# A Strassen gate/up projection moved from float32r to scaled fp16 sums

## The chip, the cores and the metric

The kernel runs on one core of a Trainium2 chip. The metric is device time in microseconds (us) of one execution. A core's engines run side by side, each taking its own instructions in order: TensorE (PE; its weight loads are listed as PEld), VectorE (DVE), ScalarE (ACT), GpSimd (POOL) and SyncE (SP, which here only issues DMA). Matmul results land in PSUM banks; other data lies in SBUF.

## The reference, cut to what matters

```python
# S = 2048 rows, D = 1024, F = 3584, 32 heads; inputs in bfloat16, scaled by 0.05
xn  = layernorm(x)
s   = linear_attention(xn, wqkv) @ wo            # phi(q) phi(k)^T v, normalised
g   = silu( (silu(xn @ w_gate) * (xn @ w_up)) @ w_down )
out = x + s * g
```

The two products `xn @ w_gate` and `xn @ w_up` ("gate/up") are the largest part.

## The kernel before

The kernel goes through these stages: layer norm, keys and values; the "query stage" (queries, attention and the output projection, four blocks of 512 rows; block 0 is the first, and its numerators are computed between the query products of the next); then two passes over 1,024 rows each, a pass being gate/up followed by down. Weights stream in. Gate/up uses one level of Strassen's method (Winograd's form): a group of 256 columns of `w_gate` or `w_up` is cut into 2x2 blocks, and seven products of sums of blocks stand in for eight. Each product is four matmuls of 512 columns, so a group is 28 matmuls, there are 28 groups in a pass, and a pass is 784 matmuls.

The weights' sums T1 to T4, the activations' sums S1, S2, S3 and a copy of one plain block (A22, which meets T4) are kept in float32r, a 32-bit format that TensorE multiplies; S4 and the plain operands are 16-bit. The T sums are made in pass 1 on GpSimd, stored to DRAM in 32 bits, and loaded again in pass 2:

```python
def t_pair():
    return [tp.tile([P, 2, HK, P], F32R, name="T%d" % k, tag="T") for k in range(2)]   # tp: 8 buffers
def emit_T(key, w):
    b11, b12 = w[:, 0:HK, 0:P], w[:, 0:HK, P:2 * P]
    b21, b22 = w[:, HK:DC, 0:P], w[:, HK:DC, P:2 * P]
    ...
    nc.gpsimd.tensor_tensor(out=T1, in0=b12, in1=b11, op=ALU.subtract)
    nc.gpsimd.tensor_tensor(out=T2, in0=b22, in1=T1, op=ALU.subtract)
    ...
...
# the products of a group, first half; y_, x_ and zw are PSUM banks
prod(y_[:], lambda k: T2[:, k, :], lambda k: S2[:, k, :], True)
prod(x_[:], lambda k: w[:, k, 0:P], lambda k: x1[:, k, :], True)
prod(zw[:, 0, :], lambda k: T3[:, k, :], lambda k: S3[:, k, :], True)
prod(zw[:, 1, :], lambda k: T1[:, k, :], lambda k: S1[:, k, :], True)
nc.scalar.copy(out=s1[:], in_=x_[:])
nc.vector.tensor_tensor(out=s2[:], in0=y_[:], in1=s1[:], op=ALU.add)
nc.vector.tensor_tensor(out=s3[:], in0=zw[:, 0, :], in1=s2[:], op=ALU.add)
```

The end of a row block, in the last sweep of down. `io` holds a block of 128 rows of `x` and of `s`, and takes one of the eight buffers of the pool of T:

```python
io = tp.tile([P, 2, D], BF16, name="io", tag="T")
xres, s_in = io[:, 0, :], io[:, 1, :]
nc.sync.dma_start(out=xres, in_=x2[r0:r0 + P, :])
nc.sync.dma_start(out=s_in, in_=s_dram[r0:r0 + P, :])
...                                                  # the matmuls of this row block
nc.scalar.activation(out=sy[:], in_=ys[(t, cc)][...], func=ACT.Silu)
nc.vector.tensor_tensor(out=sy[:], in0=sy[:], in1=s_in[:, cs], op=ALU.mult)
nc.vector.tensor_tensor(out=xres[:, cs], in0=sy[:], in1=xres[:, cs], op=ALU.add)
eng = nc.sync if last else nc.gpsimd
eng.dma_start(out=out2[r0:r0 + P, cs], in_=xres[:, cs])
```

Of the kernel before, what the change touches and what calls it, by code (L numbers as in the profile page):

```python
# [21 lines left out]
def kernel(  # L22
# [39 lines left out]
    NPREP = 12  # L62

# [9 lines left out]
    wgu = ctx.enter_context(tc.tile_pool(name="wgu", bufs=3))  # L73
    tp = ctx.enter_context(tc.tile_pool(name="tp", bufs=8))
# [19 lines left out]
    make_identity(nc, ident[:])  # L94
    mask = persist.tile([P, P], FP32, name="mask")
# [25 lines left out]
    t_drams = {}  # L121
# [29 lines left out]
    def emit_Q(b, g):  # L151
        if b not in pqT_tiles:
            pqT_tiles[b] = blk12.tile([P, G, TB], BF16, name="pqT", tag="pqT")
        pqT = pqT_tiles[b]
        btok = slice(b * TB, (b + 1) * TB)
        q_ps = ps2.tile([P, TB], FP32, name="q_ps", tag="B2")
        for dc in range(DC):
            nc.tensor.matmul(q_ps[:], lhsT=wq_sb[:, dc, g * P:(g + 1) * P], rhs=xn_ap(dc, btok),  # L158
                             start=(dc == 0), stop=(dc == DC - 1))
        emit_phi(phiw, q_ps[:], pqT[:, g, :], TB, in_place=True, act=b > 0 or g % 2 == 1)  # L160

    NPASS = NB // 2
    passes = list(range(NPASS - 1, -1, -1))
    w_seq = []
    for p in passes:
        for fg in range(NFG):
            w_seq.append((p, "g", fg))
            w_seq.append((p, "u", fg))
        for sw in range(2):
            for q in range(FC // 2):  # L170
                w_seq.append((p, "d%d" % sw, q))
    w_tiles = {}
    w_next = [0]
    n_slot = [0]
    first_gate = [None]

    def w_slot():
        t = wgu.tile([P, DC, FW], BF16, name="w_sb", tag=("wg_sb" if n_slot[0] % 2 == 0 else "wu_sb"))
        n_slot[0] += 1
        return t  # L180

    def load_gu(t, kind, k, after=None):
        d = nc.sync.dma_start(out=t[:], in_=(wg_v if kind == "g" else wu_v)[:, :, k * FW:(k + 1) * FW])
        gate([d], after, sync=True)

    def load_w(after=None):
# [6 lines left out]
        if kind[0] == "d":  # L193
            nc.sync.dma_start(out=t[:].rearrange("p a b -> p (a b)").rearrange("p (k n) -> p k n", k=2),
                              in_=wd_v[:, 2 * k:2 * k + 2, :])
        else:
            load_gu(t, kind, k, after or first_gate[0])
# [6 lines left out]
    t_tiles = {}  # L204

    def t_pair():
        return [tp.tile([P, 2, HK, P], F32R, name="T%d" % k, tag="T") for k in range(2)]

    def emit_T(key, w):
        b11, b12 = w[:, 0:HK, 0:P], w[:, 0:HK, P:2 * P]  # L210
        b21, b22 = w[:, HK:DC, 0:P], w[:, HK:DC, P:2 * P]
        ta, tb = t_pair()
        T2, T1, T3, T4 = ta[:, 0], ta[:, 1], tb[:, 0], tb[:, 1]
# [4 lines left out]
        g = key[1:]  # L218
        if g not in t_drams:
            t_drams[g] = [dram.tile([P, 2, HK, P], FP32, name="t%d_%s%d" % (k, key[1], key[2])) for k in range(2)]  # L220
            for src, dst in zip((ta, tb), t_drams[g]):
                nc.gpsimd.dma_start(out=dst[:], in_=src[:].bitcast(FP32))
        t_tiles[key] = (T1, T2, T3, T4)

    def load_T(key):
        ta, tb = t_pair()
        for dst, src in zip((ta, tb), t_drams[key[1:]]):
            gate([nc.sync.dma_start(out=dst[:].bitcast(FP32), in_=src[:])], first_gate[0], sync=True)
        t_tiles[key] = (ta[:, 1], ta[:, 0], tb[:, 0], tb[:, 1])

    gkeys = [(passes[0], kd, fg) for fg in range(NFG) for kd in ("g", "u")]
    prep_q = deque(gkeys[2:2 + 2 * NPREP:2] + gkeys[0:2])

    def prep(n, after=None):
        for _ in range(n):
            if not prep_q:
                return
            key = prep_q.popleft()
            t = w_slot()
            load_gu(t, key[1], key[2], after)  # L240
            emit_T(key, t)
            if key in gkeys[0:2]:
                w_tiles[key] = t
            else:
                t_tiles.pop(key)

    kvz_ps = [psA.tile([P, GPT, NDW], FP32, name=f"kvz{j}", tag="A") for j in range(NJ)]
    with ExitStack() as p1:
# [8 lines left out]
        p1_man.enter_context(tc.manual_schedule(engines={mybir.EngineType.PE, mybir.EngineType.DVE,  # L257
                                                         mybir.EngineType.Activation, mybir.EngineType.Pool,
                                                         mybir.EngineType.SP}))
        NXP = (NT + 1) // 2  # L260
        xp_tiles = [wgu.tile([P, 2, D], BF16, name="xp", tag=("wg_sb" if k % 2 == 0 else "wu_sb"))
                    for k in range(NXP)]

        def x_ap(i):
            return xp_tiles[i // 2][:, i % 2, :]
# [170 lines left out]
        for k in range(NWARM):  # L436
            nc.tensor.matmul(wps[:], lhsT=warm[:, 0:P], rhs=warm[:], start=True, stop=True)
        emit_stats(0)
# [30 lines left out]
        for i in range(2, NT):  # L469
            for c in range(NCH):  # L470
# [5 lines left out]
                emit_Bev(i, c)  # L476
                if c % 2 == 1:
# [8 lines left out]
            if i >= 8:  # L486
                prep(1)
        emit_C(NT - 1)
        ps1.close()
        ps2 = p12.enter_context(tc.tile_pool(name="ps2", bufs=5, space=PSUM, reuse_waits="tile"))  # L490
        for g in range(G):
            emit_Q(0, g)
            if g % 4 == 3:
# [4 lines left out]
    p2_man.enter_context(tc.manual_schedule(engines={mybir.EngineType.PE, mybir.EngineType.DVE,  # L498
                                                     mybir.EngineType.Activation, mybir.EngineType.Pool,
                                                     mybir.EngineType.SP}))  # L500
    for j in range(NJ):
        g0 = j * GPT
        ng = min(GPT, G - g0)
        nc.vector.tensor_tensor(out=KVZ[:, g0:g0 + ng, 0:P], in0=kvz_ps[j][:, 0:ng, 0:P],
                                in1=mask[:, None, :].to_broadcast([P, ng, P]), op=ALU.mult)
        nc.vector.tensor_tensor(out=KVZ[:, g0:g0 + ng, P:P + HPG],
                                in0=kvz_ps[j][:, 0:ng, P:P + 1].to_broadcast([P, ng, HPG]),
                                in1=sel[:, None, :].to_broadcast([P, ng, HPG]), op=ALU.mult)

    s_sums = {}  # L510

    def emit_Ssum(p):
# [4 lines left out]
        S1, S2, S3, A22 = [sp.tile([P, HK, TB], F32R, name="S%d" % k, tag="S%d" % k) for k in range(4)]  # L517
        S4 = sp.tile([P, HK, TB], F16, name="S4", tag="S4")
# [4 lines left out]
        nc.scalar.copy(out=A22[:], in_=a22)  # L523
        s_sums[p] = (S1, S2, S3, S4, A22)

    with ExitStack() as p2:
# [82 lines left out]
        for b in range(NB):  # L609
            q = [q_item(b + 1, g) for g in range(G)] if b + 1 < NB else []  # L610
            sl = sh(b - 1, 0) + sh(b - 1, 1) if b > 0 else []
            body = q[:2] + mix(q[2:], sl)
            at = (1, 4, 7, 10) if len(body) > 12 else ((1, 3, 5, 7) if b == 0 else (0, 1, 2, 3))
# [9 lines left out]
        prep(len(prep_q))  # L623
# [5 lines left out]
    with ExitStack() as p3:  # L629
        kp = p3.enter_context(tc.tile_pool(name="p3k", bufs=8, reuse_waits="tile"))  # L630
        cp_ = p3.enter_context(tc.tile_pool(name="p3c", bufs=1, reuse_waits="tile"))
        hp = p3.enter_context(tc.tile_pool(name="p3h", bufs=1, reuse_waits="tile"))
# [14 lines left out]
        def emit_a(key):  # L647
            p = key[0]
            w, (T1, T2, T3, T4) = w_tiles[key], t_tiles[key]
            S1, S2, S3, S4, A22 = s_sums[p]  # L650
            x1 = xn_blk_tiles[2 * p]
            y_ = pps.tile([P, TB], FP32, name="yb", tag="s")
# [7 lines left out]
            nc.scalar.copy(out=s1[:], in_=x_[:])  # L660
            nc.vector.tensor_tensor(out=s2[:], in0=y_[:], in1=s1[:], op=ALU.add)  # L661
            nc.vector.tensor_tensor(out=s3[:], in0=zw[:, 0, :], in1=s2[:], op=ALU.add)  # L662
            grp[key] = [x_, zw, s2, s3, None]

        def emit_c22(key):
            p, kind, fg = key
            x_, zw, s2, s3, _ = grp[key]
            if kind == "g":
                dst = s3[:]
            else:  # L670
                c = cp_.tile([P, 4, TB], FP32, name="cu", tag="cu")
                grp[key][4] = c
                dst = c[:, 3, :]
            nc.vector.tensor_tensor(out=dst, in0=zw[:, 1, :], in1=s3[:], op=ALU.add)

        def emit_b(key, last=False):
            w, (T1, T2, T3, T4) = w_tiles[key], t_tiles.pop(key)
            S1, S2, S3, S4, A22 = s_sums[key[0]]
# [4 lines left out]
            prod(zw[:, 0, :], lambda k: T4[:, k, :], lambda k: A22[:, k, :], False)  # L683
# [4 lines left out]
        def emit_evac(key, h):  # L688
            p, kind, fg = key
            x_, zw, s2, s3, c = grp.pop(key)  # L690
            if kind == "g":
                c = xnp.tile([P, 4, TB], FP32, name="sg", tag="xn8")
                sg_tiles[(p, fg)] = c
            nc.vector.tensor_tensor(out=c[:, 1:3, :], in0=zw[:], in1=s2[:, None, :].to_broadcast([P, 2, TB]),  # L694
                                    op=ALU.add)
            if kind == "g":
                nc.scalar.activation(out=c[:, 3, :], in_=s3[:], func=ACT.Silu)
                nc.scalar.activation(out=c[:, 1:3, :], in_=c[:, 1:3, :], func=ACT.Silu)  # L698
                nc.scalar.activation(out=c[:, 0, :], in_=x_[:], func=ACT.Silu)
# [139 lines left out]
```

## Time and profile before

The time is 801.97 us, the median of three runs (801.56 to 803.89). The profiled execution spans 799.1 us on the core. The stages, cut at the starts of matmuls, are:

| stage | us |
|---|---|
| start, keys and values | 128.74 |
| query stage | 117.80 |
| gate/up, pass 1 | 177.15 |
| down, pass 1 | 96.50 |
| gate/up, pass 2 | 177.15 |
| down, pass 2 (to the end of its last matmul) | 96.85 |
| after the last matmul's end | 4.90 |

The next fence has the page's totals of the kernel before: busy time of each engine, its share of the span and its instructions, and under it the shares of the chain of work that ended last.

```profile
PE 790.2 (99%) x3787; PEld 431.3 (54%) x3787; DVE 453.0 (57%) x739; ACT 232.9 (29%) x384; POOL 215.5 (27%) x357
PE 96%; DVE 2%; ACT 0%; DMA 0%; issue 0%; DVEq 0%; ACTq 0%
```

TensorE is the bound: busy in 99% of the span, and 96% of the chain.

Next are four of the stages of the kernel before (query, gate/up of pass 1, gate/up of pass 2, and what follows the last matmul), one line each: window, its length in us, then busy us (and instructions) of PE, PEld, DVE, ACT and POOL, the granted clock, the DMA engines' busy share, and GB/s.

```profile
128.74:246.54 117.80, 117.80 (x644) 57.45 (x641) 73.88 (x188) 69.86 (x120) 41.10 (x43) 1.00 0.64 176
246.54:423.69 177.15, 177.15 (x787) 112.85 (x786) 120.22 (x137) 47.34 (x72) 76.68 (x81) 1.00 0.78 250
520.19:697.35 177.16, 177.16 (x787) 112.86 (x786) 121.66 (x141) 44.67 (x71) 1.49 (x3) 1.00 0.81 265
794.20:799.10 4.90, 0.00 (x1) 0.00 (x0) 2.07 (x5) 0.66 (x2) 0.00 (x0) 0.76 0.25 80
```

In both gate/up stages PE is busy for the whole length, so they can only become shorter by matmuls that follow each other sooner. Which ones could, the groups by line and shape show (kernel before; operation, output<-inputs, shapes, count | busy us, mean ns of one | idle time before them):

```profile
L641 PE MATMUL yb<-S,T 128*128 128x512 f32 x224 | 71.5, 441 | 0.0
L641 PEld LDWEIGHTS zw<-S,T 128*128 128x128 f32 x672 | 126.4, 188 | 32.3
L641 PEld LDWEIGHTS <-w_sb 128*128 128x128 bf16 x672 | 56.8, 98 | 83.1 <-issue 30.5
```

A weight load takes 188 ns in float32r and 98 ns in 16 bits. One group of 28 matmuls, on TensorE's timeline of the kernel before (start us, busy us, engine, line, operation, output<-inputs, shape, count; `yb` is the product with T2 and opens a group):

```profile
395.54 1.28 PE L641 MATMUL yb<-S,T 128*128 128x512 f32 x4
396.67 1.04 PE L641 MATMUL xb<-xnT,w_sb 128*128 128x512 bf16 x4
397.35 3.12 PE L641 MATMUL zw<-S,T 128*128 128x512 f32 x12
400.31 1.04 PE L641 MATMUL zw<-S,w_sb 128*128 128x512 f16 x4
401.18 1.03 PE L641 MATMUL xb<-xnT,w_sb 128*128 128x512 bf16 x4
401.86 0.58 PE L641 MATMUL yb<-S,T 128*128 128x512 f32 x1
```

From one `yb` to the next are 401.86 - 395.54 = 6.32 us. Four 16-bit matmuls take 0.86 to 0.87 us from start to start (400.31 to 401.18).

The end of the kernel before, on the same kind of timeline (SPq is the issuing of DMA by SyncE):

```profile
785.96 10.74 SPq L766 DMA_DIRECT2D out_dram<-io  x9
795.91 0.42 DVE L764 TENSOR_TENSOR io<-sy,io 128x256 bf16<-128x256 f32 x1
```

SyncE issues nothing but the nine stores; all loads of `io` were issued long before. The last VectorE instruction starts at 795.91 us, 1.7 us after the last matmul ended at 794.20.

### The profile page before, as it was taken

The page shows a single profiled execution, that of the slowest core. Times are in us where ns is not written, and L with a number is a line of the kernel's source. Part 1 is how long each engine was busy: PE and PEld are TensorE (multiplying, and loading weights), DVE is VectorE, ACT ScalarE, POOL GpSimd, SP SyncE. Part 2 cuts the span into 40 slices and gives each one's busy share as a digit, 9 for nine tenths or more (in the row PEclk, how much of TensorE's full clock was granted, in tenths as well). Part 3 has the DMA queues.
Part 4 walks back from the last instruction along what each step waited for, and adds up shares of the span by engine and source line. Part 5 has one row for each costly group of instructions (what it writes and reads, how often), then busy time and mean ns, then how long its engine had stood idle before and what let it go on. Part 6 is the DMA issues. An engine that isn't in the chain of part 4 may idle for free.

```text
span 799.1 us, 10159 instructions
## 1 busy us (share of the span) xinstructions
PE 790.2 (99%) x3787; PEld 431.3 (54%) x3787; DVE 453.0 (57%) x739; ACT 232.9 (29%) x384; POOL 215.5 (27%) x357
## 2 busy tenths in 40 slices
PE   8999999999999999999999999999999999999997
PEld 3544444554445666666664444466666666544443
DVE  7787344774575767677672071366767667601305
ACT  4544334866534222222220030122222232200102
POOL 0576799055005443535710020100000000000100
PEclk9999999999999999999999999999999999999999
DMA  9378974386478778787786457499777787744641
GB/s 321 114 175 172 300 260 187 103 207 191 133 168 275 235 244 266 230 270 232 224 304 218 151 188 284 129 324 310 239 251 253 256 251 251 253 169 137 232 131 53
DMA packets 155296, 173.68 MB, mean 217 GB/s; under 512 B 35440, under 2 KB 114672, under 8 KB 155248
## 3 DMA queue, kind: packets, MB, share of 16 engines
q1 hardware_dynamic: 143584, 136.20, 55.9%
q0 software_dynamic: 9216, 32.51, 11.5%
q10 hardware_dynamic: 2448, 4.33, 1.6%
q8 instruction: 30, 0.49, 0.2%
q14 instruction: 18, 0.15, 0.1%
HBM read 127.93 MB, written 37.75 MB: 207 GB/s over the span
## 4 chain that ended last, share of the span: by engine, by line
PE 96%; DVE 2%; ACT 0%; DMA 0%; issue 0%; DVEq 0%; ACTq 0%
PE zw L641 26%; PE kv_ps L402 13%; PE xb L641 12%; PE y_pd L726 12%; PE y_ps L726 11%; PE s_ps L578 7%; PE q_ps L158 7%; PE yb L641 7%; PE nd_ps L551 1%; PE kvz L424 1%; DVE sy L763 1%; DVE stats L321 0%; DVE io L764 0%; DMA xp<-in_A_x_dram 0%; PE tr_ps L386 0%
## 5 line engine op out<-in xcount | busy, mean ns | idle before, releaser
L641 PE MATMUL zw<-S,T 128*128 128x512 f32 x672 | 175.3, 409 | 0.0
L726 PEld LDWEIGHTS <-hT 128*128 128x128 bf16 x896 | 87.7, 98 | 105.7
L641 PEld LDWEIGHTS zw<-S,T 128*128 128x128 f32 x672 | 126.4, 188 | 32.3
L641 PE MATMUL xb<-xnT,w_sb 128*128 128x512 bf16 x448 | 115.2, 380 | 0.0
L402 PE MATMUL kv_ps<-wkv_sb,xnT 128*128 128x512 bf16 x512 | 113.6, 379 | 0.7 <-ACT r_t L139 0.5
L726 PE MATMUL y_ps<-w_sb,hT 128*128 128x512 bf16 x448 | 103.2, 379 | 0.0
L726 PE MATMUL y_pd<-w_sb,hT 128*128 128x512 bf16 x448 | 102.9, 379 | 0.0
L766 POOL DMA_DIRECT2D out_dram<-io x24 | 13.0, 540 | 332.6 <-DVE io L764 332.6
L641 PEld LDWEIGHTS <-w_sb 128*128 128x128 bf16 x672 | 56.8, 98 | 83.1 <-issue 30.5
L763 DVE TENSOR_TENSOR sy<-sy,io 128x512 f32<-128x512 f32 (+1 forms) x33 | 22.2, 672 | 137.6 <-ACT sy L762 137.4
L402 PEld LDWEIGHTS <-xnT 128*128 128x128 bf16 x512 | 49.3, 98 | 57.2 <-issue 0.7
L660 ACT COPY s<-xb 128x512 f32<-128x512 f32 x56 | 32.7, 584 | 158.4 <-PE xb L641 158.4
L214 POOL TENSOR_TENSOR T<-w_sb 128x512 fp32r<-128x512 bf16 x28 | 33.0, 1178 | 154.8 <-DMA w_sb<-in_B_w_up_dram 87.2
L661 DVE TENSOR_TENSOR s<-yb,s 128x512 f32<-128x512 f32 x56 | 38.6, 688 | 61.9 <-ACT s L660 61.9
L641 PE MATMUL yb<-S,T 128*128 128x512 f32 x224 | 71.5, 441 | 0.0
L158 PE MATMUL q_ps<-xnT,wq_sb 128*128 128x512 bf16 x256 | 58.2, 379 | 0.0
L698 ACT ACTIVATE sg<-sg 128x1024 f32<-128x1024 f32 x28 | 29.6, 1058 | 97.6 <-DVE sg L694 97.6
L641 PE MATMUL zw<-S,w_sb 128*128 128x512 f16 x224 | 58.0, 382 | 0.0
L578 PE MATMUL s_ps<-wo_sb,oT 128*128 128x512 bf16 x256 | 57.8, 379 | 0.0
L762 ACT ACTIVATE sy<-y_pd 128x512 f32<-128x512 f32 x16 | 8.7, 595 | 159.9 <-PE y_pd L726 159.9
L662 DVE TENSOR_TENSOR s<-zw,s 128x512 f32<-128x512 f32 x56 | 38.7, 692 | 26.6 <-PE zw L641 26.5
L704 DVE TENSOR_TENSOR hT<-cu,sg 128x1536 bf16<-128x1536 f32 x28 | 49.9, 1781 | 0.0
(84 smaller groups left out, 808.3 us busy)
## 6 DMA issues: line engine op xcount, KB each, us to landing
w_sb<-in_B_w_down_dram SPq DMA_DIRECT2D x56, 512.0 KB, 4.0
T<-t_g SPq DMA_DIRECT2D x52, 512.0 KB, 4.3
w_sb<-in_B_w_gate_dram SPq DMA_DIRECT2D x40, 512.0 KB, 4.8
t_g<-T POOLq DMA_DIRECT2D x28, 512.0 KB, 4.8
w_sb<-in_B_w_up_dram SPq DMA_DIRECT2D x28, 512.0 KB, 6.6
t_u<-T POOLq DMA_DIRECT2D x28, 512.0 KB, 4.8
T<-t_u SPq DMA_DIRECT2D x28, 512.0 KB, 4.8
s_dram<-s_sb ACTq DMA_DIRECT2D x16, 256.0 KB, 4.1
```

The lines of the kernel that those rows point to most:

```text
L158: nc.tensor.matmul(q_ps[:], lhsT=wq_sb[:, dc, g * P:(g + 1) * P], rhs=xn_ap(dc, btok), start=(dc == 0), stop=(dc == DC - 1))
L214: nc.gpsimd.tensor_tensor(out=T1, in0=b12, in1=b11, op=ALU.subtract)
L402: mm = nc.tensor.matmul(kv_ps[:], lhsT=xn_ap(dc, tok), rhs=wkv_sb[:, dc, c * CW:(c + 1) * CW], start=(dc == 0), stop=(dc == DC - 1))
L578: mm = nc.tensor.matmul(s_ps[:], lhsT=oT[:, c, ttok], rhs=wo_sb[:, c, cc * CW:(cc + 1) * CW], start=(c == 0), stop=(c == G - 1))
L641: nc.tensor.matmul(out, lhsT=lhs(k), rhs=rhs(k), start=(first and k == 0), stop=(k == HK - 1), skip_group_check=True)
L660: nc.scalar.copy(out=s1[:], in_=x_[:])
L661: nc.vector.tensor_tensor(out=s2[:], in0=y_[:], in1=s1[:], op=ALU.add)
L662: nc.vector.tensor_tensor(out=s3[:], in0=zw[:, 0, :], in1=s2[:], op=ALU.add)
L698: nc.scalar.activation(out=c[:, 1:3, :], in_=c[:, 1:3, :], func=ACT.Silu)
L704: nc.vector.tensor_tensor(out=hv[:, TB:4 * TB], in0=c[:, 1:4, :].rearrange("p a b -> p (a b)"), in1=sg[:, 1:4, :].rearrange("p a b -> p (a ...
L726: nc.tensor.matmul(ys[(t, c)], lhsT=h[:, fc, tt], rhs=wt[:, o:o + CW], start=(fc == 0), stop=(fc == FC - 1), skip_group_check=True)
L763: nc.vector.tensor_tensor(out=sy[:], in0=sy[:], in1=s_in[:, cs], op=ALU.mult)
```

## The change

The intent is to run all gate/up products in 16 bits. The sums go to fp16. So that they cannot overflow or lose small values in fp16's range, each group of weights is scaled by a power of two (exact) that comes from the sum of its absolute values. ScalarE takes the absolute values and sums them in each partition; a one-column TensorE matmul with a matrix of ones sums over partitions; VectorE picks the exponent by integer operations and scales the weights in place. The inverse factor `rc` is folded into the instructions that empty PSUM. The weights and their T sums lie together in one 1 MB "pack", which goes to DRAM in one store and comes back in pass 2 in one load. The order on four engines is fixed by hand throughout, the operands of the hT product go to bf16, and phi of block 0 moves towards VectorE: every second phi took three ScalarE passes and one VectorE pass, now all take one and two. The weights of down come in the same 1 MB slots, and in pass 1 the last VectorE work of a down stage is put behind the next group.

```diff
-        return [tp.tile([P, 2, HK, P], F32R, name="T%d" % k, tag="T") for k in range(2)]
+    def t_view(t):
+        v = t[:, 1].rearrange("p a b -> p (a b)").bitcast(F16).rearrange("p (t k n) -> p t k n", t=4, k=HK)
+        return [v[:, k] for k in range(4)]
+
+    def emit_st0(key, t):
+        asum = stp.tile([P, 1], BF16, name="asum", tag="asum")
 ...
+            nc.scalar.activation(out=t[:, 1]..., in_=t[:, 0]..., func=ACT.Abs, accum_out=asum[:])
 ...
+    def emit_st1(key, ps):
+        nc.tensor.matmul(ps, lhsT=ones[:], rhs=st_tiles.pop(key)[:], start=True, stop=True, ...)
 ...
+    def emit_st2(key, t):
+        ...   # three one-column VectorE operations: mask the exponent, rc = it, cs = 1 / it
+        nc.vector.tensor_scalar(out=w, in0=w, scalar1=cs_all[:, c:c + 1], scalar2=None, op0=ALU.mult)
 ...
+        pk = dram.tile([P, 2, DC, FW], BF16, name="pk_%s%d" % key[1:])
+        nc.gpsimd.dma_start(out=pk[:], in_=t[:])
 ...
-        S1, S2, S3, A22 = [sp.tile([P, HK, TB], F32R, ...) for k in range(4)]
-        nc.scalar.copy(out=A22[:], in_=a22)
+        S1, S2, S3, S4 = [sp.tile([P, HK, TB], F16, ...) for k in range(4)]
 ...
-        emit_phi(phiw, q_ps[:], pqT[:, g, :], TB, in_place=True, act=b > 0 or g % 2 == 1)
+        emit_phi(phiw, q_ps[:], pqT[:, g, :], TB, in_place=True, act=b > 0)
 ...   # emit_a, and the same in emit_c22 and emit_evac
-            nc.scalar.copy(out=s1[:], in_=x_[:])
-            nc.vector.tensor_tensor(out=s2[:], in0=y_[:], in1=s1[:], op=ALU.add)
+            nc.scalar.activation(out=s1[:], in_=x_[:], func=ACT.Copy, scale=rc)
+            nc.vector.scalar_tensor_tensor(out=s2[:], in0=y_[:], scalar=rc, in1=s1[:], op0=ALU.mult, op1=ALU.add)
 ...   # the end of a row block; iop has two buffers
-                io = tp.tile([P, 2, D], BF16, name="io", tag="T")
+                io = iop.tile([P, 2, D], BF16, name="io", tag="io")
 ...   # gate/up of pass 1: the sum of group i+3 is put between the two halves of the products
+                pipe(i + 4, i + 3)
                 emit_b(keys[i], i == n - 1)
```

Half of the 28 groups are prepared in pass 1 itself, and the other half earlier, in preparation steps beside the key/value and the query stage (half of the groups were prepared early in the kernel before too, but without the scale).

## The prediction

> **What bounds the kernel now.** TensorE. The page's first part shows PE busy 790.2 us of a 799.1 us span, clock 1.0 throughout; the chain of waits is 96% PE. Stages, from the timeline of matmul starts: start-up and key/value 128.7 us, query/attention/output 117.8, gate/up 177.15, down 96.5, gate/up 177.15, down 96.9, then some 5 us of tail. A 16-bit matmul of 512 columns starts 216 ns after the one before in every stage, the warm pace in the Trainium skill ("TensorE: Matmul & The Clock Gate", Back-to-back issue gap). So only the float32r products of gate/up (T1 to T4, 16 of a group's 28 matmuls) have something to give. Their weight loads take 188 ns against 98 for 16-bit weights (groups by form); the same page, Weight-path perf modes, says the fast load is not used for FP32, and this trace agrees. They start 226 to 239 ns apart, and the first pair of a float32r run costs some 420 ns, partly given back by a 28 ns start before it. A group takes 6.32 us where 28 x 0.216 is 6.04.
>
> **What the change removes.** Each pass becomes 784 x 0.2157 = 169.1 us: -8.05 us, twice: **-16.1 us**, all on the critical path. It also cuts DMA (pass 2 loads 1 MB per group, not 1.5), the 1,536-element hT product (1.78 us in float32; about half with 16-bit operands) and the four S sums (2.3 to 2.8 us each): DVE and DMA are not the bound, so these earn nothing directly.
>
> **What it adds.**
> - 28 one-column matmuls with a weight load each. 132-column matmuls with a load each pace at 59 ns here; I charge 60: +1.7 us.
> - 28 ScalarE Abs passes (about 1.9 us, as the A22 copy of that size), 28 DVE scalings (about 0.7 to 1.1 us) and small ops. They fit in the key/value stage. In the query stage ScalarE already runs 1.8 us per 1.73 us product; two Abs passes put it behind near the second block: about +1 us.
> - In pass 1, 14 of those sums write into the yb bank and wait for s2 (xb end, ScalarE copy 0.58, DVE 0.69). By my count s2 is ready within 0.1 us of TensorE's arrival: 0 to 1 us in total. T sums on GpSimd (4 x 1.18 us) finish about 1.5 us before T2 is needed.
> - The io tiles go from 8 buffers to 2. In the last tail, rows of blocks 2 and 3 load only once the results of blocks 0 and 1 have landed (1.7 us), and that load takes 2.5 to 3.6 us: DVE waits, and the kernel ends about +2 us later. Earlier tails hide it.
>
> **Sum.** 802.0 - 16.1 + 1.7 + 1 + 0.5 + 2 = about 791; I say **790.5 us**, 8 in 10 between **785.5 and 796**. Faster by over 2%: 0.12; within 2%: 0.86; slower: 0.02.
>
> **What would show it.** All gate/up matmuls 216 ns apart with 98 ns weight loads; passes of 169 to 171 us, pass 1 longer by 1 to 2 us; one-column sums of some 60 ns; DMA share in pass 2 down from 0.81 to about 0.55; DVE idle in the last 15 us, ended by io loads, and some 7 us after the last matmul start.
>
> **What would make it wrong.** 16-bit products slower than 216 ns; a one-column sum stalling the pipe by several hundred ns; GpSimd late with T in pass 1; stalls of several us from Abs in ScalarE's queue. The other way: fast io loads and no stalls, about 787.

## The result, and the profile after

The changed kernel takes 795.17 us (median of 4 runs, 794.08 to 796.34), the kernel before 802.15 us in the runs then at hand. The ratio is 0.9904, with a 95% interval of 0.9885 to 0.9924: 0.96% faster. Ratios here are the mean time of one kernel's runs over that of the other's of the same rounds, so not quite the ratio of the medians quoted. The result lies inside the predicted range, 4.7 us above the predicted point and only 0.8 us below the range's upper end; the slowest of the four runs, 796.34, lies beyond it.

The totals and the chain of the changed kernel:

```profile
PE 778.4 (98%) x3815; PEld 360.2 (45%) x3815; DVE 473.1 (60%) x856; ACT 282.4 (36%) x430; POOL 198.4 (25%) x329
PE 47%; DVE 2%; DMA 1%; issue 0%; ACT 0%; SPq 0%; DVEq 0%
```

There are 28 more matmuls, the sums. The chain could be followed back only to about 396 us here, so its shares add up to half of the span; what it holds is again nearly all PE. DVE and ACT became busier (453 to 473 and 233 to 282 us).

The stages that answer to those above:

```profile
129.54:249.82 120.28, 119.03 (x650) 57.70 (x648) 79.41 (x220) 74.01 (x123) 42.48 (x43) 1.00 0.61 177
249.82:420.77 170.95, 170.54 (x799) 77.01 (x798) 133.35 (x193) 76.40 (x100) 71.21 (x70) 1.00 0.66 232
517.72:686.93 169.21, 169.21 (x786) 76.71 (x784) 122.02 (x145) 48.50 (x71) 2.16 (x4) 1.00 0.52 188
784.04:792.80 8.76, 0.00 (x0) 0.00 (x0) 4.89 (x9) 0.66 (x2) 0.00 (x0) 0.79 0.37 120
```

Gate/up of pass 2 fell by 7.95 us to 169.21, which is 0.2158 us for each of its 784 matmuls: every product at the 16-bit pace. Pass 1 fell by only 6.20, the query stage grew by 2.48, and the end of the kernel by 3.8. In the query stage PE now has 1.25 us idle in its window, where it had none. Of the 2.48 us, 0.19 is no work but the cut: in the kernel before, the first float32r product of a pass starts 28 ns after the 16-bit matmul in front of it, in the changed kernel 216 ns after, so a little of each pass's gain is booked in the stage before it.

The weight loads and one product of the changed kernel, by line and shape:

```profile
L682 PE MATMUL yb<-S,w_sb 128*128 128x512 f16 x224 | 57.5, 379 | 0.0
L682 PEld LDWEIGHTS <-w_sb 128*128 128x128 f16 x896 | 86.6, 98 | 105.0 <-issue 2.1 <-POOL w_sb L248 0.4
```

All 896 loads of T take 98 ns now, as the trace of before promised for 16 bits. A piece of a group in pass 2, on TensorE's timeline of the changed kernel, has 0.86 to 0.87 us per four matmuls, whatever the operands:

```profile
527.21 1.03 PE L682 MATMUL yb<-S,w_sb 128*128 128x512 f16 x4
528.08 1.03 PE L682 MATMUL xb<-xnT,w_sb 128*128 128x512 bf16 x4
528.94 1.89 PE L682 MATMUL zw<-S,w_sb 128*128 128x512 f16 x8
530.67 1.03 PE L682 MATMUL zw<-xnT,w_sb 128*128 128x512 bf16 x4
```

What pass 1 pays for the scale: the timeline of the changed kernel around one sum.

```profile
280.24 0.75 DVE L704 SCALAR_TENSOR_TENSOR s<-yb,rc_all,s 128x512 f32<-128x512 f32 x1 [0.55 <-ACT s L703]
281.04 0.16 PE L229 MATMUL yb<-asum,ones 128*128 128x1 bf16 x1
281.07 1.02 PE L682 MATMUL zw<-xnT,w_sb 128*128 128x512 bf16 x4
```

The sum holds TensorE's stream for 0.03 us (281.04 to 281.07; 25 to 29 ns for one sum in all stages, its own weight load included; some 25 ns net, as the matmuls after it start a little closer). But it writes into the `yb` bank, which the instruction of line 704 reads, so it must wait until that one has ended at 280.99. That one came later than its counterpart, as the groups show. First the kernel before, ScalarE's copy of `x_` and VectorE's sum after it, then the same two in the changed kernel:

```profile
L660 ACT COPY s<-xb 128x512 f32<-128x512 f32 x56 | 32.7, 584 | 158.4 <-PE xb L641 158.4
L661 DVE TENSOR_TENSOR s<-yb,s 128x512 f32<-128x512 f32 x56 | 38.6, 688 | 61.9 <-ACT s L660 61.9
```

```profile
L703 ACT ACTIVATE s<-xb,rc_all 128x512 f32<-128x512 f32 x56 | 38.2, 683 | 118.3 <-PE xb L682 73.3 <-issue 45.0
L704 DVE SCALAR_TENSOR_TENSOR s<-yb,rc_all,s 128x512 f32<-128x512 f32 x56 | 42.0, 751 | 67.1 <-ACT s L703 67.1
```

With a factor read from SBUF per partition, ScalarE's instruction takes 99 ns longer (it also changed from a copy to an activation) and VectorE's 63 ns (its operation changed too, but the kernel before has SCALAR_TENSOR_TENSOR instructions of this size without such a factor, which take 685 ns). The Trainium skill ("ScalarE: Activation LUTs", What ACT_TABLE_LOAD costs) says that each such pointer operand adds about 93 ns to a ScalarE activation; this trace agrees with 99. TensorE waits some 48 ns at each of 11 sums, and 0.25 and 0.17 us at two others, where two groups prepared in pass 1 follow each other. Between these two, a wait of 0.47 us is not at a sum: the first `xb` product of a group waits for its bank, which a VectorE instruction that writes hT (line 754) still reads. Together that is 1.4 us. The view of TensorE's waits from gate/up of pass 1 to gate/up of pass 2 lists only the wait at `xb`, and of it only the part in which TensorE was idle (engine, tile, line, what it waited for: us in total, times, the longest):

```profile
PE xb L682 <- DVE hT L754: 0.3, 1, 0.3
```

The query stage: TensorE's waits in the changed kernel, in the same form.

```profile
PE st_ps L229 <- DVE rden L594: 1.1, 2, 0.6
```

Two sums of this stage wait in block 0 for a PSUM bank that VectorE has not yet emptied of the numerators before; the kernel before has no such wait. By the starts of matmuls these two cost 0.71 us each, and the numerator products around them another 0.6 us in all.

The end of the changed kernel, on the timelines of SyncE's DMA issues and of VectorE:

```profile
775.79 1.67 SPq L816 DMA_DIRECT2D out_dram<-io  x2
778.89 0.34 SPq L795 DMA_DIRECT2D io<-in_A_x_dram  x1
779.33 0.37 SPq L816 DMA_DIRECT2D out_dram<-io  x1
779.76 0.42 SPq L796 DMA_DIRECT2D io<-s_dram  x1
780.57 0.33 SPq L816 DMA_DIRECT2D out_dram<-io  x1
783.66 0.34 SPq L795 DMA_DIRECT2D io<-in_A_x_dram  x1
783.32 0.69 DVE L813 TENSOR_TENSOR sy<-sy,io 128x512 f32<-128x512 f32 x1 [2.77 <-DMA io<-s_dram]
787.17 0.69 DVE L813 TENSOR_TENSOR sy<-sy,io 128x512 f32<-128x512 f32 x1 [1.11 <-DMA io<-s_dram]
789.75 0.42 DVE L814 TENSOR_TENSOR io<-sy,io 128x256 bf16<-128x256 f32 x1
```

With two `io` buffers, the `x` of the third row block can be issued only when the stores of the first have landed (778.89), and its `s` only after one more store, which stood before it in SyncE's queue (779.33, then 779.76: some 0.5 us). For the fourth row block SyncE can issue `x` only at 783.66, when the second block's last store, issued at 780.57, has landed (783.59: 3.0 us, where the first block's stores took 1.7). VectorE then waits 2.77 and 1.11 us for `s`, and its last instruction starts at 789.75, which is 5.7 us after the last matmul ended (1.7 before).

### The profile page after: what moved, and what is told of

It reads as the page before. It is cut to its first block, busy times and chain, and to the rows that moved or that the text cites. A ratio compares the mean times of both kernels' runs of the same rounds, so it can differ in the third digit from the quotient of the medians.

```text
span 792.8 us, 10141 instructions
## 1 busy us (share of the span) xinstructions
PE 778.4 (98%) x3815; PEld 360.2 (45%) x3815; DVE 473.1 (60%) x856; ACT 282.4 (36%) x430; POOL 198.4 (25%) x329
## 4 chain that ended last, share of the span: by engine, by line
PE 47%; DVE 2%; DMA 1%; issue 0%; ACT 0%; SPq 0%; DVEq 0%
PE zw L682 14%; PE y_pd L779 12%; PE y_ps L779 11%; PE xb L682 7%; PE yb L682 3%; DVE cu L744 0%; DMA io<-s_dram 0%; DMA out_dram<-io 0%; DVE io L814 0%; DVE sy L813 0%; DVE hT L754 0%; DVE s L704 0%; ACT sy L810 0%; SPq L795 0%; PE yb L229 0%
## 5 line engine op out<-in xcount | busy, mean ns | idle before, releaser
L682 PEld LDWEIGHTS <-w_sb 128*128 128x128 f16 (+1 forms) x1568 | 152.4, 98 | 184.8 <-issue 2.7
L682 PE MATMUL zw<-S,w_sb 128*128 128x512 f16 x672 | 163.3, 379 | 0.0
L704 DVE SCALAR_TENSOR_TENSOR s<-yb,rc_all,s 128x512 f32<-128x512 f32 x56 | 42.0, 751 | 67.1 <-ACT s L703 67.1
L703 ACT ACTIVATE s<-xb,rc_all 128x512 f32<-128x512 f32 x56 | 38.2, 683 | 118.3 <-PE xb L682 73.3
L248 POOL TENSOR_TENSOR w_sb<-w_sb 128x512 f16<-128x512 bf16 x28 | 32.2, 1151 | 180.7 <-DVE w_sb L241 109.7
L682 PE MATMUL yb<-S,w_sb 128*128 128x512 f16 x224 | 57.5, 379 | 0.0
L682 PE MATMUL zw<-xnT,w_sb 128*128 128x512 bf16 x224 | 57.4, 379 | 0.0
L224 ACT ACTIVATE w_sb<-w_sb 128x2048 bf16<-128x2048 bf16 x28 | 53.3, 1904 | 0.0
L705 DVE SCALAR_TENSOR_TENSOR s<-zw,rc_all,s 128x512 f32<-128x512 f32 x56 | 42.0, 751 | 9.2 <-PE zw L682 5.9
L744 DVE SCALAR_TENSOR_TENSOR cu<-zw,rc_all,s 128x1024 bf16<-128x1024 f32 x28 | 35.9, 1283 | 6.7 <-PE zw L682 4.7
```

The source lines that it names most:

```text
L224: nc.scalar.activation(out=t[:, 1].rearrange("p a b -> p (a b)"), in_=t[:, 0].rearrange("p a b -> p (a b)"), func=ACT.Abs, accum_out=asum[:])
L682: nc.tensor.matmul(out, lhsT=lhs(k), rhs=rhs(k), start=(first and k == 0), stop=(k == HK - 1), skip_group_check=True)
L703: nc.scalar.activation(out=s1[:], in_=x_[:], func=ACT.Copy, scale=rc)
L704: nc.vector.scalar_tensor_tensor(out=s2[:], in0=y_[:], scalar=rc, in1=s1[:], op0=ALU.mult, op1=ALU.add)
L705: nc.vector.scalar_tensor_tensor(out=s3[:], in0=zw[:, 0, :], scalar=rc, in1=s2[:], op0=ALU.mult, op1=ALU.add)
L744: nc.vector.scalar_tensor_tensor(out=d12, in0=zw[:], scalar=rc, in1=s2[:, None, :].to_broadcast([P, 2, TB]), op0=ALU.mult, op1=ALU.add)
```

## The experiments

Ten kernels ran, in three calls, each beside the kernel before on the same chip (medians of before 803.43, 802.03 and 801.82 us). All gave correct results. The theory was: what the dtype gained (16 us) was partly given back in three separate places, the end of the kernel (two `io` buffers), the query stage, and the sums of pass 1, the latter two both caused by the scale. Stage lengths below are cut from each trace in the same way. The start with keys and values varied from 128.7 to 132.5 us between runs of kernels that are alike there. No run explains this; it is treated as chance here, and it makes single totals uncertain by a us or two, while the stages repeat to a few hundredths.

| us | start + kv | query | gate/up 1 | down 1 | gate/up 2 | down 2 | after the start of the last matmul |
|---|---|---|---|---|---|---|---|
| before | 128.74 | 117.80 | 177.15 | 96.50 | 177.15 | 96.86 | 5.32 |
| after | 129.54 | 120.28 | 170.95 | 96.95 | 169.21 | 97.11 | 9.10 |
| a1_tail_io4 | 131.02 | 120.28 | 170.94 | 96.95 | 169.21 | 97.11 | 5.07 |
| a2_outq | 132.50 | 120.27 | 170.94 | 96.95 | 169.21 | 97.11 | 12.95 |
| a3_before_fp16 | 131.05 | 117.99 | 169.21 | 96.69 | 169.21 | 96.86 | 5.33 |
| a4_noscale | 129.89 | 117.99 | 169.21 | 96.95 | 169.21 | 97.11 | 9.24 |
| b1_defer | 128.88 | 120.67 | 170.95 | 96.95 | 169.21 | 97.11 | 9.31 |
| b2_noabs | 129.47 | 119.72 | 170.94 | 96.95 | 169.21 | 97.11 | 9.22 |
| b3_before_io2 | 129.85 | 117.80 | 177.15 | 96.92 | 177.15 | 96.86 | 7.48 |
| b4_best | 131.24 | 120.68 | 169.54 | 96.69 | 169.21 | 96.86 | 5.08 |
| c1_moved | 131.21 | 118.19 | 169.54 | 96.69 | 169.21 | 96.86 | 5.10 |
| c2_phiback | 129.55 | 122.61 | 170.95 | 96.94 | 169.21 | 97.11 | 9.12 |

The last column overlaps the one before it by the last matmul, some 0.3 to 0.4 us.

### a1_tail_io4: four `io` buffers in the last sweep

```diff
-                io = iop.tile([P, 2, D], BF16, name="io", tag="io")
+                if last:
+                    if t % 2 == 0:
+                        io2 = xnp.tile([P, 2, 2, D], BF16, name="io2", tag="xn8")   # space that is free by then
+                    io = io2[:, t % 2]
+                else:
+                    io = iop.tile([P, 2, D], BF16, name="io", tag="io")
```

> The changed kernel; only in the last sweep of the last pass the four io tiles come from the space of two dead xnT tiles, so no io load waits for a store. Theory (the two-buffer io pool sets the tail): the time from the last matmul's start to the end falls from 8.8 us to about 5.2 us as before the change, all else the same: about 791.5 us, ratio to the changed kernel 0.995. Rival (the tail is long because the stores themselves land late at the end): no more than 1 us gained, about 794.5 us.

Measured: 792.3 us (791.79 to 793.01), ratio 0.9864 (0.9846 to 0.9881). The end fell from 9.10 to 5.07 us, all other stages of the change stayed. In total it is only 2.9 us faster than the changed kernel, as its start took 1.5 us longer. VectorE's waits for `s` are gone, and SyncE issues nine stores in a row as it did before. SyncE's issues and VectorE's waits at the end of this kernel:

```profile
777.26 10.74 SPq L821 DMA_DIRECT2D out_dram<-io  x9
DVE sy L818 <- ACT sy L815: 33.4, 2, 32.6
```

The two buffers cost 3.8 to 4.0 us; the mechanism is shown.

### a2_outq: the last stores on ScalarE's queue

```diff
-                            eng = nc.sync if last else nc.gpsimd
+                            eng = nc.scalar if last else nc.gpsimd
```

> The changed kernel; the last sweep's stores are issued from ScalarE's queue instead of SyncE's, the io pool still has two buffers. Theory (each load waits for a store to land): the order of the queue is worth only the 0.4 to 0.9 us by which a load stood behind an issue that waited for VectorE: gain of 0.5 to 1 us, 794 to 795 us, VectorE still idle for io loads. Rival (loads stand behind waiting stores in one queue): most of the 3.9 us comes back, about 791.5 us.

Measured: 798.55 us, ratio 0.9939 (0.9919 to 0.9959), slower than the changed kernel: the end took 12.95 us instead of 9.10. (The totals alone don't settle it: the two intervals overlap, and the profiled run's start was 3 us longer.) Both expectations missed. ScalarE's waits at the end of this kernel:

```profile
ACT sy L810 <- DVE io L814: 14.4, 8, 1.9
```

The issue of a store waits for VectorE's result in ScalarE's own queue, and the next Silu stands behind it, eight times. The Trainium skill ("DMA: Bandwidth & Descriptors", Anatomy of one DMA — SWDGE (gpsimd) path) says that a DMA's semaphore wait happens on the sequencer that issues it; the section describes DMAs issued by GpSimd, and the 14.4 us of waiting Silus show the same for ScalarE. The run built a new wait and so does not tell how much of the end was queue order and how much was the landing of stores.

### a3_before_fp16: the kernel before, sums in fp16, no scale, nothing else

```diff
-        return [tp.tile([P, 2, HK, P], F32R, name="T%d" % k, tag="T") for k in range(2)]
+        return [tp.tile([P, 2, HK, P], F16, name="T%d" % k, tag="T") for k in range(2)]
-        S1, S2, S3, A22 = [sp.tile([P, HK, TB], F32R, name="S%d" % k, tag="S%d" % k) for k in range(4)]
+        S1, S2, S3, A22 = [sp.tile([P, HK, TB], F16, name="S%d" % k, tag="S%d" % k) for k in range(4)]
```

(The DRAM copies of T go to fp16 as well.)

> The kernel before, with T and S sums in fp16 instead of float32r and nothing else: no scale, no one-column sums, old pools. Theory: each gate/up pass takes 169.2 us instead of 177.15, nothing else moves: 802.1 - 15.9 = about 786 us, ratio 0.980; the result may round somewhat differently but should pass. Rival (part of the gain is given back elsewhere whenever TensorE gets faster): a pass of 169.2 but 790 us or more in all.

Measured: 787.81 us (787.47 to 788.87), ratio 0.981 (0.9792 to 0.9827). Each gate/up pass takes 169.21 us; down 2 and the end are as before. The query stage and down 1 are 0.19 us longer, though nothing in them was edited: that is the cut told of above (the first product of a pass starts 216 ns after the matmul in front of it here, 28 ns in the kernel before). So the dtype alone is worth 2 x (7.94 - 0.19) = 15.5 us, and the traces from the start of the query stage to the end agree (670.4 us before, 654.9 here). Everything else in the change together costs 7 to 8 us more than it brings (7.4 by the medians, 8.3 by the same stretch of the traces). Gate/up of pass 1, and the weight loads of this kernel:

```profile
249.04:418.25 169.21, 169.21 (x786) 76.71 (x784) 120.25 (x137) 47.27 (x72) 74.33 (x78) 1.00 0.60 181
L641 PEld LDWEIGHTS <-T 128*128 128x128 f16 x896 | 87.7, 98 | 105.7
```

It gives up the protection of fp16's range, which these inputs do not need (the result was correct).

### a4_noscale: the changed kernel without the scale

```diff
+    nc.vector.memset(rc_all[:], 1.0)
     def emit_st0(key, t):
+        return
 ...   # and so emit_st1, emit_st2: no Abs, no one-column sum, no exponent, no scaling
```

> The changed kernel without its scale: no Abs pass, no one-column sums, no bit operations, no in-place scaling; the factor is a constant 1. Everything else (fp16, packs, pools, order) stays. Theory: the scale's work costs what the gaps between matmul starts show, 1.7 us in gate/up pass 1, 2.2 us in the query stage and 0.2 us in key/value: about 4 us less than the changed kernel, 791 us; the tail stays at 8.8 us. Rival (the query stage's loss comes from moving all of block 0's phi to VectorE, not from the scale): only about 2 us less, 793 us, and the query stage still near 120 us.

Measured: 790.93 us, ratio 0.9846 (0.9829 to 0.9863). Gate/up of pass 1 is 169.21 us (it lost its 1.74), and the query stage, as below, 117.99:

```profile
129.89:247.88 117.99, 117.99 (x644) 57.54 (x642) 71.88 (x192) 63.76 (x111) 33.32 (x33) 1.00 0.55 159
```

PE is busy for all of it again. The scale costs 1.74 + 2.29 = 4.0 us by the trace of these two stages, its sums included. The theory held. Phi on VectorE in block 0 is still there, so moving phi is not the cause by itself. The end is unchanged (9.24), as it should be.

### b1_defer: preparation steps of the query stage one work item later

```diff
+        pend = [False]
         def nd_item(b, t):
 ...
-                    prep(1)
+                    pend[0] = True
 ...
                 f()
+                if pend[0]:
+                    pend[0] = False
+                    prep(1)
```

> The changed kernel; in the query stage each one-column sum comes one work item later (after the next query or output product) instead of right behind the numerator products. Theory (the sum waits for a PSUM bank that VectorE has not yet read): the two waits of 0.72 us go, query stage from 120.3 to 118.3 or 118.8 us, in all 793 to 793.7 us. Rival (VectorE or ScalarE is behind in that stage, so the loss only moves to the next product that needs a bank): stage still above 119.8 us.

Measured: 796.25 us, ratio 0.9922 (0.9905 to 0.9939); query stage 120.67, not shorter. The waits of the sums went, and other waits of the same size came: TensorE's waits in this kernel's query stage are

```profile
PE nd_ps L589 <- DVE o_blk L597: 1.6, 3, 0.6
```

The theory that the PSUM bank of the sum was the cause fell, and the rival's range (above 119.8) was met. The reading that is left, and that c1 tests, is that VectorE is late, and whichever matmul first needs its result pays.

### b2_noabs: Abs replaced by a one-element operation

```diff
-            nc.scalar.activation(out=t[:, 1]..., in_=t[:, 0]..., func=ACT.Abs, accum_out=asum[:])
+            nc.scalar.activation(out=asum[:], in_=t[:, 0, 0, 0:1], func=ACT.Copy, scale=0.0, bias=1.0)
```

> The changed kernel; the 2,048-element Abs pass is replaced by a one-element ScalarE op that writes 1, so the sums, the scaling and their order stay (every group gets the same power of two; the result is still right). Prediction's reason (two Abs passes put ScalarE behind in the query stage): that stage falls to about 118.3 us. Theory (the bank, VectorE): it stays within 0.5 us of 120.3 us. In gate/up pass 1 both expect the 48 ns waits in front of the sums to stay, since they wait for s2.

Measured: 795.72 us, ratio 0.9918 (0.9899 to 0.9936); query stage 119.72, only 0.56 less; neither expectation was met, the theory's by 0.1 us. One of the two waits stays in full, the other falls from 0.71 to 0.29 us:

```profile
PE st_ps L228 <- DVE rden L593: 0.6, 1, 0.6
```

So the 1.9 us Abs passes on ScalarE, which the prediction named, make up a quarter of the query stage's loss, not all of it. What is left after this removal, and is gone in a4, are the sums themselves (7 of them, 0.18 us) and what comes of the small operations and the scaling on VectorE (795 ns for one group in the changed kernel).

### b3_before_io2: the kernel before with two `io` halves used in turn

```diff
-                io = tp.tile([P, 2, D], BF16, name="io", tag="T")
+                if last:
+                    if t == 0:
+                        io2 = xnp.tile([P, 2, 2, D], BF16, name="io2", tag="xn8")
+                    io = io2[:, t % 2]
+                else:
+                    io = tp.tile([P, 2, D], BF16, name="io", tag="T")
```

> The kernel before; only in the last sweep of the last pass its io tiles are two buffers used in turn, so the loads of rows 2 and 3 wait for stores. Theory: the tail after the last matmul start grows from 5.3 to about 9.1 us, in all +3.8 us, ratio 1.0047, with VectorE idle for io loads twice. Rival (the tail's loss needs something else of the change): less than 1.5 us.

Measured: 804.85 us, ratio 1.0038 (1.0014 to 1.0061). The end grew from 5.32 to 7.48 us: +2.2, not +3.8. VectorE's waits there:

```profile
DVE io L769 <- issue: 1.3, 1, 1.3
DVE io L769 <- DMA io<-in_A_x_dram: 0.9, 1, 0.9
```

It now waits for `x`, not for `s`. One tile split in two is a weaker reuse than two tiles: in this kernel the load of `s` was issued as soon as the multiplication that read the old `s` was over, without waiting for a store; in the changed kernel both loads wait for the whole old tile, store included. Fewer buffers in the old kernel thus lengthen its end too, but this run is no exact copy of the change's reuse. (It also lost 0.4 us in down 1, where a matmul waited for a weight load, as no other run of this kernel did.)

### b4_best: four repairs together

This is a1 and b1, and in addition: the sums of pass 1 stand one product later (after T4's), one more group is prepared early, and in the last group of a pass the product that frees the bank of down's first results comes first.

```diff
-    NPREP = 12
+    NPREP = 13
             prod(zw[:, 0, :], lambda k: T4[:, k, :], lambda k: a22[:, k, :], False)
+            if mid_st[0] is not None:
+                mid_st[0]()               # the one-column sum
+                mid_st[0] = None
             prod(zw[:, 1, :], lambda k: w[:, HK + k, P:2 * P], lambda k: S4[:, k, :], False)
```

> The changed kernel with its four losses mended: io tiles of the last sweep in dead xnT space; query-stage sums one item later; pass 1 sums after the T4 product instead of before it, and all gate groups but none more prepared ahead (13 instead of 12); in a pass's last group the product that frees the bank the down stage needs first comes first. Theory: -3.8 (tail), -1.5 to -2 (query), -0.6 to -1.4 (pass 1), -0.5 (down starts): gate/up pass 1 169.6 us, tail 5.1 us, in all 787.5 to 789 us, ratio to before 0.981 to 0.983, level with the kernel before in plain fp16. Rival: removing one wait uncovers another, 790 us or more.

Measured: 790.21 us (788.77 to 790.7), ratio 0.9849 (0.9832 to 0.9866); a little over the expected range and just inside the rival's. Gate/up 1 is 169.54 (only the sums themselves are left: 13 x 25 ns = 0.33), each down stage lost its 0.25, the end is 5.08. The query stage stayed at 120.68, as b1 had shown. For down this also settles a small term of the result: each down stage of the changed kernel lost 0.25 us at its tenth matmul, whose bank waited for a VectorE instruction that stood behind another of the last group.

### c1_moved: b4, with no preparation in block 0

```diff
             emit_Q(0, g)
-            if g % 3 == 1:
-                prep(1)
 ...
-                if t % 2 == 1:
-                    prep(1)
+                if b >= 1:
+                    pend[0] = True
```

> The mended kernel of the last call (tail, pass 1 and down starts mended, sums deferred by one item), with the preparation steps taken out of block 0 of the query stage (three between its query products, two beside its numerators) and put into blocks 1 and 2, one per row instead of one per two rows. Theory (VectorE is behind in block 0: phi of all eight query products, the KVZ masks and four scalings fall there, and numerator products wait for banks that it has not yet read): the query stage falls from 120.7 to 118.0 to 118.4 us, in all 2.3 to 2.6 us less than before this step, 787.5 to 788 us, ratio to before 0.982. Rival (the same work makes VectorE late wherever it stands in the stage): stage stays above 119.5 us.

Measured: 787.17 us (786.43 to 788.98, five runs), ratio 0.9806 (0.9783 to 0.9829). The query stage is

```profile
131.21:249.40 118.19, 117.50 (x638) 57.76 (x649) 80.71 (x224) 75.94 (x125) 47.95 (x48) 1.00 0.73 203
```

as short as without the scale, up to 0.2 us, which is what its 8 sums themselves take (25 ns each), although VectorE and ScalarE do as much as in the changed kernel (80.7 and 75.9 us against 79.4 and 74.0). (Some matmul records are missing from this trace, so PE's busy time is too low; the waits of the trace show none of the query stage's sums waiting.) Not the amount of the scale's work, but its place in block 0 was the cost: this move alone took b4's 120.68 us to 118.19. This is the fastest kernel that keeps the scale; it is faster than both kernels of the case and level with a3 (by the 2% rule "unclear" too, between same and faster).

### c2_phiback: the changed kernel, phi of block 0 split between ScalarE and VectorE again

```diff
-        emit_phi(phiw, q_ps[:], pqT[:, g, :], TB, in_place=True, act=b > 0)
+        emit_phi(phiw, q_ps[:], pqT[:, g, :], TB, in_place=True, act=b > 0 or g % 2 == 1)
```

> The changed kernel with one thing of it undone: in block 0 of the query stage every second phi goes by ScalarE again (three ScalarE passes and one VectorE pass instead of one and two), as before the change. It takes 4 x 0.7 us from VectorE and gives ScalarE 4 x 1.2 us. Theory (VectorE's backlog of block 0 is what costs): the stage falls from 120.3 to about 118.3 to 119.3 us. Rival (the backlog is shared: ScalarE with its Abs passes becomes the late one): the stage stays at 120 us or gets longer.

Measured: 797.36 us, ratio 0.9934 (0.9912 to 0.9956); query stage 122.61, longer by 2.3. In block 0 VectorE now waits for ScalarE:

```profile
DVE pqT L135 <- ACT q_ps L134: 6.1, 7, 1.5
```

In the changed kernel the same wait came once, 1.0 us. With Abs in its queue, ScalarE had no room for its half of phi; giving it to VectorE was right, and left VectorE with the backlog that b1 met. Taking phi off VectorE does not help; taking the preparation out of block 0 does.

## Why the prediction was right or wrong

The range held, narrowly; the point was 4.7 us too low. Of the costs only the sums were charged too high, the others were too low or missing, and the gain was 0.6 us too high. The terms, as predicted and as the traces show them:

| term | predicted | trace | shown by |
|---|---|---|---|
| products in 16 bits, two passes | -16.1 | -15.5 | pass 2, a3 |
| 28 one-column sums | +1.7 | +0.7 | gaps, some 25 ns net each |
| waits in pass 1 | +0.5 (0 to 1) | +1.4 | a4, b4 |
| waits in the query stage | +1 | +2.1 | a4, c1 |
| end of the kernel | +2 | +3.8 | a1 |
| start of the down stages | not foreseen | +0.5 | b4 |
| start, keys and values, without its sums | 0 | +0.6 | taken as chance, within 128.7 to 132.5 |
| sum | -10.9 | -6.4 | |

The span itself fell by 799.1 - 792.8 = 6.3 us, the median by 7.0. (Terms are read from cuts at matmul starts; they close to about 0.1 us. The query stage's 2.48 us hold 0.19 of the cut, 0.18 of sums and 2.11 of waits; pass 1's 1.74 hold 0.36 of sums and 1.38 of waits. Cut by stage, the two passes fell by 15.9 us; 0.4 of that came back in the stages before them.)

- "16-bit matmul of 512 columns starts 216 ns after the one before": right. So was the reading of the weight loads: 188 ns became 98, which is what the Trainium skill ("TensorE: Matmul & The Clock Gate", Weight-path perf modes) leads one to expect when the operand is no longer FP32. This was the whole gain, and a3 gets it alone. (The section that the prediction names for the 216 ns calls them the gap of an isolated matmul; see the last section. The prediction took them for a stream, and the runs bear it out. Its 16.1 us overlooked that the start after 28 ns, which it had seen, shortens the stage before.)
- "132-column matmuls with a load each pace at 59 ns here; I charge 60": mis-sized. One-column sums take 25 to 29 ns. A shape of 132 columns was taken as the stand-in for one of 1 column. The same skill page (Back-to-back issue gap) gives an issue floor of about 25 ns for 1 to 64 columns, and this trace agrees; it would have been the better source.
- "By my count s2 is ready within 0.1 us": right for 11 sums (48 ns late), but two others waited 0.17 and 0.25 us, and an `xb` product, which the prediction did not look at, 0.47. The count used the 0.58 and 0.69 us of the old instructions; with the factor they take 0.68 and 0.75.
- "two Abs passes put it behind near the second block: about +1 us": a loss in the query stage was rightly expected, with too small a size and only part of the cause. Abs is 0.56 of it (b2); the rest goes when the scale's same work is done later (c1), and the waits are waits for VectorE, which the prediction did not name.
- "The io tiles go from 8 buffers to 2 ... about +2 us later": the mechanism was right (a1), the size too small. The prediction named the landing of stores, for both blocks, and the load behind it. It put the landing at 1.7 us, and the store that the fourth block waited for took 3.0 (780.57 to 783.59), beside two loads; and it missed that `x` and `s` are issued one after the other, with a store's issue between them for the third block. VectorE waited 2.77 and then 1.11 us, 3.9 in all.
- "DMA share in pass 2 down from 0.81 to about 0.55": 0.52, and as said it earned nothing. The hT product halved (1,781 to 948 ns), also without effect on TensorE.

What stays open: the split of the end's 3.8 us between queue order and landing. No run separated them (a2 did not tell it); the trace of the changed kernel speaks for landing, as the last wait of VectorE was ended by loads that SyncE held back for a landing store alone, and queue order shows as some 0.5 us for the third block. Open too is how the remaining 1.5 us of the query stage's waits divides among the small operations and the scaling on VectorE, which no run took away one by one.

## What to carry to other kernels

When one engine is the bound, a change of its operands' type pays what the change in its own pace says, and the rest of a large change is a list of ways to give that back: here 15.5 us were gained by a few lines (a3), and some 8.5 us were lost to buffers, to helpers' work and to its place in the order. Before adding work to idle engines, look for the stretch in which their results are awaited soon, and put it elsewhere: the same work cost 2.3 us with its early steps in block 0, and 0.2 us with them in blocks 1 and 2. When buffers are cut, look at the last use of each in the kernel, where nothing hides a load that must wait for a store.

## What the Trainium skill lacked or had wrong

- "TensorE: Matmul & The Clock Gate" has no pace for float32r products. Here a mixed group of 16 float32r and 12 16-bit matmuls took 6.32 us, an all-16-bit one 6.04, with weight loads of 188 and 98 ns.
- The same page (Back-to-back issue gap) gives about 131 ns as the sustained spacing at 512 columns and calls its formula (216 ns) the isolated case. In every sustained 16-bit stream here the spacing was 216 ns: 784 matmuls in 169.21 us. (Elsewhere the same page has 215.7 ns for back-to-back matmuls, and this is what the runs show.)
- "VectorE: DVE Perf Modes" gives 691 ns for an fp32 tensor_tensor of 512 columns (here 688), and neither it nor "DVE: scalar operands, raw-bit mode, write accounting and state across instructions" gives the time that a per-partition factor adds: 751 ns here, +63.
- "DMA: Bandwidth & Descriptors" says where a DMA's wait happens, but not what this does to a compute engine that issues: stores issued by ScalarE held its Silus for 14.4 us in eight waits (a2), and the end of the kernel took 12.95 us, against 9.10 with SyncE issuing.
